# Later scatters and sums, an expert matrix in seven pieces, one gather moved up

## Chip, core and metric

One core of one Trainium2 chip runs the whole program in one launch. The metric is the device time of the run in microseconds (us); the median before is 1282.26 us over three runs (1281.8 to 1287.79).

## What is computed

Three layers in a row, on 4608 tokens of width 512. The gate weights are scaled so that the routing decides clearly.

```python
# 1. attention inside chunks of 64 positions, 8 heads of 64, softmax, no mask
scores = scale * q_c @ k_c.T;  x = softmax(scores) @ v_c         # -> x: 4608 x 512
# 2. dense layer
h = np.maximum(x @ w_in, 0.0);  x = h * h @ w_out                # 512 -> 2048 -> 512
# 3. one of 8 experts for each token
logits = x @ w_gate + modality_bias[modality_id]
e_idx = np.argmax(logits, axis=1);  gate_w = softmax(logits)[e_idx]
for e in range(8):
    mask = e_idx == e
    h = np.maximum(x[mask] @ w1[e], 0.0)                         # 512 -> 1024
    out[mask] = gate_w[mask, None] * (h @ w2[e])                 # 1024 -> 512
```

## The kernel before

**Numbers.** Every fp32 value of a matmul is split into a high and a low fp16 part, and a product is three fp16 matmuls: high by high, high by low, low by high. ScalarE writes the high part, and VectorE or GpSimd the low part as a difference. Most 2 x 2 blocked products go in seven block products instead of eight, so sums and differences of blocks are formed first.

**Stages.** The 4608 tokens are 36 tiles of 128. Nine groups (`supers`) of four tiles go through the dense layer: a first matmul (`mm1` for the first three groups, `prod` for the six others, L620), squares (`square`, whose low part is GpSimd's at L662), and a second matmul in four quarters for each tile (`mm2`, L809), which reads the squares in `bigs[2]` and the weights `w_out` in `bigs[1]`. Attention of the coming tiles runs beside it. Then 25 to 32 pairs, each of 256 tokens of one expert, run through `pair_mm1` (L1189) and `pair_mm2` (L1257). Pair 0's first matmul (`first1`) is slipped between the quarters of the last two tiles.

**Routing.** Behind each tile's last quarter a chain of calls has planned offsets: `x2_evac`; `x2_tr` (a DMA transpose at L829 and a store to DRAM, both on SyncE's queue); `route_a` (a small matmul `lp`, L837, on the transposed tile, then the expert of each token); `route_b` (places within the expert); `route_c`, which computes the gate weight on VectorE and ends with an indirect DMA (L879) on GpSimd's queue that scatters token number and weight into the DRAM table `meta`. Behind tile 31 (`SEEN - 1`), `map_a1`, `meta_gather` and `map_a2` make the index lists of the first four pairs from the tiles seen so far; behind tile 35, `map_b1` to `map_b3` make those of the rest.

**Expert weights.** The two most used experts' matrices are made ready during the dense layer: 16 blocks, each with four quarters loaded into `raw`, seven splits (`part_split`, in the order of `ORDER`), four sums or differences of quarters on GpSimd (`part_sum`, L310) that overwrite a quarter already split, and fourteen stores into the DRAM table `wsp`. `part_plan` writes the list `order_` with times; the splits are 3.43 planned us apart ((742.1 - 96 - 262)/112). The items are emitted strictly in the order of the list, each when it is due and the engines' planned backlog is low; the sum that reads a quarter's last value is followed by the split of the result.

**Hand-over.** After the last quarter of tile 35 the first expert's second matrix (x = 1, 3.67 MB) is loaded from `wsp` into `bigs[1]` by four DMAs that ScalarE issues (`early_w`, L1069): one block, then twice or three times two blocks. Then pair 1's seven first products run (`run1(1, n)`), then pair 0's second matmul, then both kinds alternate, pair 2's first product standing in slot 11. The gather of pair 2 (`x_gather`, L1108, two indirect loads on GpSimd's queue into `bigs[2]`) is emitted at the start of this stage, its two DMA transposes (`x_tr`, L1116, SyncE) in slot 4, its sums (`x_sum0` on VectorE, `x_sum1` on ScalarE and GpSimd) in slots 8 and 10. A slot is one block product, planned at 1.33 us.

**What sets the order.** The program is emitted in one order for all engines by a planner: each step of TensorE advances a planned time T, and before it all events due by T are emitted (`flush`), subject to dependences and to planned backlogs. Each engine then runs its own instructions strictly in that order and waits on semaphores. So where an event is emitted decides what stands behind it in its engine's queue.

Of the kernel before, what the change touches and what calls it, by code (L numbers as in the profile page):

```python
# [12 lines left out]
U32 = mybir.dt.uint32  # L13
AF = mybir.ActivationFunctionType
ALU = mybir.AluOpType
# [7 lines left out]
EARLY = 4  # L23
# [2 lines left out]
FULL = 4  # L26
GSP = 36
WO_O = 4
READY = 2


@with_exitstack
def kernel(
# [18 lines left out]
    NTILE = NT // 128  # L52
# [8 lines left out]
    SEEN = NTILE - 4  # L61
# [16 lines left out]
    meta = dram.tile([MROWS, 2], F32, name="meta")  # L78
    wsp = dram.tile([E, 2, 128, 14336], F16, name="wsp")

    bigs = [big.tile([128, 16384], F16, name=f"big{i}") for i in range(3)]
# [36 lines left out]
    def ts2(out, in0, s1, s2, op0, op1=None, eng=None):  # L118
        if op1 is None:
            (eng or nc.vector).tensor_scalar(out=out, in0=in0, scalar1=s1, scalar2=None, op0=op0)  # L120
        else:
            (eng or nc.vector).tensor_scalar(out=out, in0=in0, scalar1=s1, scalar2=s2, op0=op0, op1=op1)
# [112 lines left out]
    def narrow_hi(which, c):  # L235
        hw = wl[which, c][0]
        if which == 1 and c >= WO_O:
            if "r" not in whp:
# [62 lines left out]
    def part_of(m):  # L301
        return m // (4 * READY), m // 4 % READY, m % 4 * 256

# [9 lines left out]
    SUMS = {0: ((0, 1, 0),), 1: ((1, 2, 1), (2, 2, 0)), 5: ((3, 2, 3),)}  # L313
# [15 lines left out]
    def choose_regs():  # L329
        mp["regs"] = [nc.sync.value_load(first[0:1, k:k + 1], min_val=0, max_val=E - 1) for k in range(READY)]  # L330

# [48 lines left out]
    order_ = []  # L380
# [4 lines left out]
    def part_plan(t0, dt):  # L385
        for m in range(8 * READY):
            t = t0 + 7 * dt * m
            if m == 0:
                order_.extend((t - 8.0 + b, part_load, (m, b)) for b in range(4))
            for n, (k, b) in enumerate(ORDER):  # L390
                at_ = t + n * dt
                order_.append((at_, part_split, (7 * m + n, m, k, b)))
                order_.extend((at_ + 0.3 + 0.1 * x, part_sum, (m, *v, ALU.subtract)) for x, v in enumerate(SUMS.get(n, ())))
                order_.extend((at_ + 0.5 * l + 2.0, part_store, (m, k, l)) for l in range(2))
                nxt = {2: 0, 3: 1, 5: 2, 6: 3}.get(n)
                if nxt is not None and m + 1 < 8 * READY:
                    order_.append((at_ + 3.5, part_load, (m + 1, nxt)))
# [398 lines left out]
    x2 = {}  # L796
# [73 lines left out]
    def route_c(i):  # L870
        a = x2[i]
        di, se = a["di"], a["se"]
        mt = sm_p.tile([128, 2], F32, tag="mt", name="mt")
        nc.gpsimd.tensor_copy(out=mt[:, 0:1], in_=tok[:, i:i + 1])
        ga = sm_p.tile([128, 1], F32, tag="ga", name="ga")
        ts2(ga, se, 1e-9, None, ALU.add)
        nc.vector.reciprocal(out=ga, in_=ga)
        ts2(mt[:, 1:2], ga, a["ui"][:, 0:1], SWG / (SW1 * SW2), ALU.mult, ALU.mult)
        nc.gpsimd.indirect_dma_start(  # L879
            out=meta[:, :], out_offset=bass.IndirectOffsetOnAxis(ap=di[:, 0:1].bitcast(U32), axis=0),  # L880
            in_=mt, in_offset=None,
        )
        x2.pop(i)

    mp = {}
    pair = {}
# [47 lines left out]
    def spread_pairs(ti, fs, base, n):  # L934
        for s in range(n):
            pair[base + s] = [(ti[:, h, s:s + 1], fs[:, h, s:s + 1]) for h in range(2)]
# [79 lines left out]
    def map_a2():  # L1016
        ti, fs = meta_spread(EARLY, "a")
        spread_pairs(ti, fs, 0, EARLY)
        row = const.tile([1, PAIRS], F32, name="row")
        ep = ps_r.tile([128, 512], F32, tag="r", name="epa")  # L1020
        nc.tensor.matmul(ep[0:1, 0:EARLY], lhsT=mp["eha"][:, 0:1], rhs=id_h[:, 0:EARLY], start=True, stop=True)
        nc.vector.tensor_copy(out=row[:, 0:EARLY], in_=ep[0:1, 0:EARLY])
        mp["row"] = row
        mp["rg", 0] = changes(EARLY, "a")
# [42 lines left out]
    def load_part(x, e, k, eng=None, **kw):  # L1067
        a, b = (2048 * n for n in GROUPS[k])
        (eng or nc.sync).dma_start(out=bigs[x][:, a:b], in_=wsp[bass.ds(e, 1), x, :, a:b].rearrange("a p c -> (a p) c"), **kw)  # L1069

    def early_w(x, k):
        assert stored[0] >= 28 * READY * (x + 1), (x, k, stored)
        eng = (nc.sync, nc.scalar)[x]
        if k == 0:
            mp["ew", x] = eng.value_load(mp["rga"][0:1, 0:1], min_val=0, max_val=E - 1)
        load_part(x, mp["ew", x], k, eng)

    def late_w(x, p, n):
        if p >= PAIRS or n not in [b - 1 for _, b in GROUPS] or (x, p, n) in gone:
# [72 lines left out]
    def once(fn, *a):  # L1152
        if a[-1] < PAIRS and (fn, *a) not in gone and a[-1] in pair:
            gone.add((fn, *a))
            fn(*a)
# [152 lines left out]
    def at_time(t, fn, *a):  # L1308
        push(t, [(t, fn, a)], 0)
# [91 lines left out]
    def plan_start():  # L1401
# [53 lines left out]
        for c in range(KF):  # L1455
            op(("old", c), "DMA", 1.35, [("osl", c - 4)], load_w, 1, c)
            op(("ona", c), "ACT", 0.67, [("old", c), ("onb", c - 1), ("nb", KF - 1)] + ([("nr", 3), "nw"] if c >= WO_O else []), narrow_hi, 1, c)
            op(("ond", c), "DVE" if (1, c) in ND_DVE else "ACT", 0.42 if (1, c) in ND_DVE else 0.67, [("old", c)], narrow_lo, 1, c)
# [86 lines left out]
    T = 0.0  # L1545
    span = []
    for su, (b0, nt, sb) in enumerate(supers):
        ta = T
        if su < HALVED:
            for c in range(KF):  # L1550
                steps.append((T, mm1, (su, c)))
                T += STEP
        else:
            for n in range(KF // 4):
                for k in (1, 5, 2, 6, 4, 3, 7):
                    steps.append((T, prod, (su, n, k)))
                    T += STP
        span.append((ta, T))
        TM1 = T
        for t, qq in M2 if su == 0 else [(t, qq) for t in range(nt) for qq in range(4)]:  # L1560
            steps.append((T, mm2, (su, t, qq)))
            T += STEP
            i = b0 + t
            if i >= NTILE - 2 and (i, qq) < (NTILE - 1, 3):
                steps.append((T, first1, (4 * (i - NTILE + 2) + qq,)))
                T += 1.33
            if qq < 3:
                continue
            d = (4.0, 11.0, 16.0, 19.0) if i < NTILE - 1 else (4.0, 8.2, 12.0, 14.0)
            ch = [(T, x2_evac, (i,)), (T + d[0], x2_tr, (i,)), (T + d[1], route_a, (i,)), (T + d[2], route_b, (i,)), (T + d[3], route_c, (i,))]  # L1570
            if i == 3:
                ch += [(T + 22.0, choose, ()), (T + 30.0, choose_regs, ())]
            if i == SEEN - 1:
                ch += [(T + 20.0, map_a1, ()), (T + 23.0, map_a1b, ()), (T + 26.0, meta_gather, (EARLY, "a")), (T + 33.0, meta_turn, (EARLY, "a")), (T + 35.0, map_a2, ())]
                ch += [(T + 37.0 + p, once, (x_gather, p)) for p in range(2)]
                ch += [(T + 44.0 + p, once, (x_tr, p)) for p in range(2)]
                ch += [(T + 49.0 + 8 * p, once, (x_sum, p)) for p in range(2)]
            if i == NTILE - 1:
                ch += [(T + 16.0, map_b1, ()), (T + 18.0, map_b1b, ()), (T + 21.0, map_b2, ()), (T + 22.0, meta_gather, (LATE, "b")), (T + 29.0, meta_turn, (LATE, "b")), (T + 31.0, map_b3, ())]
                ch += [(T + 34.0 + p, once, (x_gather, 4 + p)) for p in range(2)]  # L1580
                ch[1:1] = [(T + 0.1 * k, early_w, (1, k)) for k in range(2, 4)]
                ch[0:0] = [(T, early_w, (1, k)) for k in range(2)]
            at_chain(ch)
        if su == len(supers) - 1:
            at_time(TM1 + 8.0, map_a1c)
            at_time(TM1 + 2.0, rest, "a", [quad(b) for b in range(4)], [slot(n) for n in range(2)])
            for k in range(4):
                at_time(TM1 + 3.0 + 2.65 * k, early_w, 0, k)
            for n in range(7):
                at_time(T - STEP + 1.33 * n, pair_s, 0, n)  # L1590
# [10 lines left out]
    for t, fn, a in plan_start():  # L1601
# [2 lines left out]
    ws = [(87.0 + 9.0 * (3 * q + n), (q, n)) for q in range(4) for n in range(3)] + [(213.0 + 6.0 * q, (q, 3)) for q in range(4)]  # L1604
    at_chain([x for (t, a), (u, b) in zip(ws, [(0.0, None)] + ws[:-1]) for x in ([(u + 4.5, w_split, b)] if b else []) + [(t, w_form, a)]]
             + [(ws[-1][0] + 6.0, w_split, ws[-1][1])])
    for n, (t, _, _) in enumerate(order_):
        at_time(t, part, n)
    with tc.manual_schedule():
# [34 lines left out]
        T = TEND  # L1644
# [43 lines left out]
        slots = []  # L1688
        side = {}

        once(x_gather, 2)
        once(x_gather, 3)
        for k, fn, q in ((4, x_tr, 2), (6, x_tr, 3), (8, x_sum0, 2), (10, x_sum1, 2), (14, x_sum0, 3), (17, x_sum1, 3), (27, x_tr, 4)):
            later(k, fn, q)
        for n in range(7):
            run1(1, n)
# [88 lines left out]
```

## Time and profile before

| | |
|---|---|
| runs | 1287.79, 1282.26, 1281.8 us, median 1282.26 |
| the profiled execution by itself | 1289.27 us, span of the trace 1287.2 us, mean granted TensorE clock 0.972 |
| busy | TensorE 1185.2 us (92%), VectorE 935.0 (73%), ScalarE 707.1 (55%), GpSimd 688.5 (53%) |
| DMA | SyncE's queue q1 117.91 MB, GpSimd's q0 20.54 MB, ScalarE's q10 3.67 MB in 576 packets |

All times in rows are us from the start of the span. PE is TensorE's matmuls, DVE VectorE, ACT ScalarE, POOL GpSimd, SP SyncE; a q behind the name (ACTq, SPq) marks the engine's sequencer issuing a DMA. A helper that records every operation of its kind has one line (L113 all ScalarE activations, L116 most of VectorE's), so tiles tell them apart. In brackets stands how long the engine was idle before an instruction and what ended it. A DMA share over 1 is possible, since packets of several queues overlap.

### The profile page before, as it was taken

The page shows a single profiled execution, that of the slowest core. Times are in us where ns is not written, and L with a number is a line of the kernel's source. Part 1 is how long each engine was busy: PE and PEld are TensorE (multiplying, and loading weights), DVE is VectorE, ACT ScalarE, POOL GpSimd, SP SyncE. Part 2 cuts the span into 40 slices and gives each one's busy share as a digit, 9 for nine tenths or more (in the row PEclk, how much of TensorE's full clock was granted, in tenths as well). Part 3 has the DMA queues.
Part 4 walks back from the last instruction along what each step waited for, and adds up shares of the span by engine and source line. Part 5 has one row for each costly group of instructions (what it writes and reads, how often), then busy time and mean ns, then how long its engine had stood idle before and what let it go on. Part 6 is the DMA issues. An engine that isn't in the chain of part 4 may idle for free. (4 is left out here: it accounts for less than half of the span.)

```text
span 1287.2 us, 33045 instructions
## 1 busy us (share of the span) xinstructions
PE 1185.2 (92%) x12910; PEld 838.3 (65%) x12910; DVE 935.0 (73%) x2031; ACT 707.1 (55%) x1392; POOL 688.5 (53%) x641
## 2 busy tenths in 40 slices
PE   5898999999989989989899899899579999999996
PEld 4443444445754854844764765755569999999995
DVE  6899797775786896885886883943477676766763
ACT  6887673674564664663664562533334555555552
POOL 4488364587573573573483572554145554455451
PEclk9899999999999999999999999999889999999999
DMA  9454523315325437436336423253925435843332
GB/s 375 151 167 129 119 50 96 63 41 124 80 71 128 114 80 156 114 99 147 95 83 162 89 67 93 64 166 74 168 41 117 91 77 163 232 92 75 85 92 58
DMA packets 188775, 144.45 MB, mean 112 GB/s; under 512 B 126586, under 2 KB 163486, under 8 KB 187058
## 3 DMA queue, kind: packets, MB, share of 16 engines
q1 hardware_dynamic: 180386, 117.91, 38.3%
q0 software_dynamic: 7632, 20.54, 5.7%
q10 hardware_dynamic: 576, 3.67, 1.1%
q8 instruction: 103, 1.69, 0.6%
q14 instruction: 78, 0.64, 0.2%
HBM read 204.06 MB, written 34.48 MB: 185 GB/s over the span
## 5 line engine op out<-in xcount | busy, mean ns | idle before, releaser
L809 PEld LDWEIGHTS <-big 128*128 128x128 f16 x1728 | 164.8, 98 | 208.6 <-POOL big L662 15.1
L809 PE MATMUL oo<-big,big 128*128 128x512 f16 x1056 | 237.8, 381 | 3.4 <-POOL big L771 3.4
L1189 PEld LDWEIGHTS <-big 128*128 128x128 f16 x3192 | 192.8, 99 | 22.0 <-issue 17.8
L809 PE MATMUL hh<-big,big 128*128 128x512 f16 x672 | 151.9, 382 | 10.3 <-POOL big L662 10.3
L1189 PE MATMUL hh<-big,big 128*128 128x128 f16 x2040 | 129.2, 220 | 9.7 <-DMA big<-big 9.7
L620 PEld LDWEIGHTS <-big 128*128 128x128 f16 x1152 | 113.5, 100 | 29.9 <-issue 14.1
L791 PE MATMUL hh<-xtall,big 128*128 128x512 f16 x576 | 129.7, 383 | 0.2 <-ACT r L113 0.2
L791 PEld LDWEIGHTS <-big 128*128 128x128 f16 x576 | 55.3, 98 | 64.6 <-issue 2.7
L116 DVE SCALAR_TENSOR_TENSOR stage<-raw,stage 128x256 f16<-128x256 f32 x112 | 76.7, 689 | 20.3 <-ACT stage L113 14.5
L310 POOL TENSOR_TENSOR raw<-raw 128x256 f32<-128x256 f32 x64 | 53.5, 836 | 67.4 <-DVE stage L116 47.6
L1257 PEld LDWEIGHTS <-xtall 128*128 128x128 f16 x840 | 80.4, 99 | 12.1 <-issue 3.1
L488 POOL TENSOR_TENSOR ee<-ee,rc 128x512 f32<-128x512 f32 x36 | 40.2, 1117 | 84.2 <-DVE rc L486 58.2
L1283 POOL DMA_INDIRECT out_dram<-raw,tib x30 | 35.2, 1172 | 92.3 <-DVE raw L116 73.2
L879 POOL DMA_INDIRECT meta<-mt,di x36 | 37.6, 1046 | 85.4 <-issue 27.2
L771 POOL TENSOR_TENSOR big<-sn,big 128x512 f16<-128x512 f32 x48 | 59.0, 1233 | 35.9 <-DVE sn L116 15.7
L1257 PE MATMUL oo<-big,xtall 128*128 128x256 f16 x600 | 75.4, 277 | 2.7 <-DVE raw L116 2.7
L662 POOL TENSOR_TENSOR big<-r,big 128x512 f16<-128x512 f32 x48 | 65.3, 1375 | 17.5 <-ACT big L113 9.7
L1150 POOL TENSOR_TENSOR big<-big 128x512 f16<-128x512 f32 x34 | 39.5, 1181 | 60.8 <-ACT big L113 60.7
L116 DVE SCALAR_TENSOR_TENSOR qkt<-qk,qkt 128x1024 f16<-128x1024 f32 x32 | 51.5, 1608 | 21.7 <-ACT qkt L113 21.2
L113 ACT ACTIVATE big<-hh 128x512 f32<-128x512 f32 x62 | 36.8, 594 | 53.7 <-PE hh L1189 46.3
L662 POOL TENSOR_TENSOR big<-sn,big 128x512 f16<-128x512 f32 x48 | 60.0, 1265 | 11.5 <-ACT big L113 10.1
L113 ACT ACTIVATE stage<-raw 128x256 f16<-128x256 f32 x112 | 45.4, 409 | 35.7 <-DMA wsp<-stage 18.5
(384 smaller groups left out, 2705.9 us busy)
## 6 DMA issues: line engine op xcount, KB each, us to landing
big<-wsp SPq DMA_DIRECT2D x111, 1024.0 KB
big<-wsp SPq DMA_DIRECT2D x37, 512.0 KB
qk<-in_qk_dram SPq DMA_DIRECT2D x34, 512.0 KB
wsp<-stage SPq DMA_DIRECT2D x224, 64.0 KB
x2d<-xs SPq DMA_DIRECT2D x36, 256.0 KB
vv<-in_v_dram SPq DMA_DIRECT2D x34, 256.0 KB
big<-in_w_in_dram SPq DMA_DIRECT2D x16, 512.0 KB
raw<-in_w_out_dram SPq DMA_DIRECT2D x16, 512.0 KB
```

Source lines behind the costliest of these rows:

```text
L113: nc.scalar.activation(out=out, in_=in_, func=func, **kw)
L116: nc.vector.scalar_tensor_tensor(out=out, in0=in0, scalar=s, in1=in1, op0=op0, op1=op1, **kw)
L310: nc.gpsimd.tensor_tensor(out=quad(out_), in0=quad(in0), in1=quad(in1), op=op)
L488: eng.tensor_tensor(out=ee, in0=ee, in1=rc.unsqueeze(2).to_broadcast([128, H, 64]), op=ALU.mult)
L620: nc.tensor.matmul(ps[:, f * 256:f * 256 + 256], lhsT=block(k, la, kk, 2 * n + f), rhs=xa(lb, kk), start=k in (1, 5, 2, 4) and f + m + kk ...
L662: nc.gpsimd.tensor_tensor(out=lo, in0=c, in1=hi, op=ALU.subtract)
L771: nc.gpsimd.tensor_tensor(out=lo, in0=q32.rearrange("p (f n) -> p f n", f=nf), in1=hi, op=ALU.subtract)
L791: nc.tensor.matmul(hp[:, q_ * n:(q_ + 1) * n], lhsT=wi[:, la, kk, f * 128:f * 128 + 128], rhs=x[:, lb, kk, :], start=i == 0, stop=i == 3 * ...
L809: nc.tensor.matmul(ps, lhsT=g[:, la, f, c:c + 128], rhs=wo[:, lb, f, :], start=f == 0 and n == 0, stop=f == KF - 1 and n == 2)
L1150: eng.tensor_tensor(out=sl[:, 2 * h:2 * h + 2], in0=s[h], in1=sh[:, 2 * h:2 * h + 2], op=ALU.subtract)
L1189: nc.tensor.matmul(ps[:, f * 128:f * 128 + 128], lhsT=WB[0][:, n, la, kk, f * 128:f * 128 + 128], rhs=xa(lb, kk), start=first and f + m + ...
L1257: nc.tensor.matmul(ps, lhsT=hb[:, la, f * 128:f * 128 + 128], rhs=WB[1][:, n, lb, f, :], start=first and f + m == 0, stop=True, skip_group ...
```

## The change

- `part_sum` is planned 2.2 us (a second one 3.3) behind its split instead of 0.3 (0.4), and the list `order_` is sorted by time.
- The scatter leaves `route_c` and becomes `route_d`, an event of its own: 6 planned us behind `route_c` for most tiles, 2 for tile 34, 0.2 for tile 31, 0.5 for tile 35.
- The second expert matrix is loaded in seven DMAs of one block each, in the order 0, 4, 1, 5, 2, 6, 3: two behind each of the first three quarters of tile 35 (`EW` = 0.8 planned us later) and one behind the last. Blocks 0 and 4 lie on the parts of `w_out` that the first quarter reads last, and so on.
- Pair 2's gather is emitted 0.5 and its transposes 6.5 planned us behind the first quarter of tile 35.
- `map_a2` goes 2 us later, and its second half, the rows that tell when an expert changes, becomes `map_a2b`, 10 us behind it; the gathers of pairs 0 and 1 go 1.5 us later.

```diff
+EW = 0.8
-                order_.extend((at_ + 0.3 + 0.1 * x, part_sum, (m, *v, ALU.subtract)) for x, v in enumerate(SUMS.get(n, ())))
+                order_.extend((at_ + 2.2 + 1.1 * x, part_sum, (m, *v, ALU.subtract)) for x, v in enumerate(SUMS.get(n, ())))
...
+    def route_d(i):
+        a = x2.pop(i)
         nc.gpsimd.indirect_dma_start(
-            out=meta[:, :], out_offset=bass.IndirectOffsetOnAxis(ap=di[:, 0:1].bitcast(U32), axis=0),
-            in_=mt, in_offset=None,
+            out=meta[:, :], out_offset=bass.IndirectOffsetOnAxis(ap=a["di"][:, 0:1].bitcast(U32), axis=0),
+            in_=a["mt"], in_offset=None,
         )
-        x2.pop(i)
...
         spread_pairs(ti, fs, 0, EARLY)
+
+    def map_a2b():
         row = const.tile([1, PAIRS], F32, name="row")
...
-        load_part(x, mp["ew", x], k, eng)
+        if x == 0:
+            load_part(x, mp["ew", x], k, eng)
+            return
+        a, e = (0, 4, 1, 5, 2, 6, 3)[k] * 2048, mp["ew", x]
+        eng.dma_start(out=bigs[x][:, a:a + 2048], in_=wsp[bass.ds(e, 1), x, :, a:a + 2048].rearrange("a p c -> (a p) c"))
...
+            if i == NTILE - 1 and qq < 3:
+                for k in range(2):
+                    at_time(T + EW + 0.1 * k, early_w, 1, 2 * qq + k)
+                if qq == 0:
+                    at_time(T + 0.5, once, x_gather, 2)
+                    at_time(T + 6.5, once, x_tr, 2)
             if qq < 3:
                 continue
-            d = (4.0, 11.0, 16.0, 19.0) if i < NTILE - 1 else (4.0, 8.2, 12.0, 14.0)
+            d = (4.0, 11.0, 16.0, 19.0, 25.0) if i < NTILE - 2 and i != SEEN - 1 else (4.0, 11.0, 16.0, 19.0, 21.0) if i < NTILE - 1 and i != SEEN - 1 else (4.0, 11.0, 16.0, 19.0, 19.2) if i < NTILE - 1 else (4.0, 8.2, 12.0, 14.0, 14.5)
...
-                ch[1:1] = [(T + 0.1 * k, early_w, (1, k)) for k in range(2, 4)]
-                ch[0:0] = [(T, early_w, (1, k)) for k in range(2)]
+                ch[1:1] = [(T + 0.1, early_w, (1, 6))]
...
+    order_.sort(key=lambda e: e[0])
...
-        once(x_gather, 2)
         once(x_gather, 3)
-        for k, fn, q in ((4, x_tr, 2), (6, x_tr, 3), (8, x_sum0, 2), (10, x_sum1, 2), (14, x_sum0, 3), (17, x_sum1, 3), (27, x_tr, 4)):
+        for k, fn, q in ((6, x_tr, 3), (8, x_sum0, 2), (10, x_sum1, 2), (14, x_sum0, 3), (17, x_sum1, 3), (27, x_tr, 4)):
```

## Rows read from the trace of the kernel before

**Rows 1.** Busy time by stretches: start:end, length, engines, PEclk, DMA share, GB/s.

```profile
880.00:892.00 12.00, 12.00 (x120) 7.75 (x119) 4.92 (x19) 3.33 (x9) 1.24 (x2) 1.00 0.01 2
892.00:896.00 4.00, 4.00 (x38) 2.58 (x37) 1.62 (x9) 1.45 (x4) 0.82 (x1) 1.00 0.52 131
902.00:912.00 10.00, 5.59 (x100) 5.47 (x99) 6.14 (x18) 3.06 (x7) 1.39 (x1) 0.94 0.90 305
912.00:917.00 5.00, 5.00 (x48) 5.00 (x48) 3.12 (x7) 3.91 (x9) 1.88 (x3) 0.50 1.49 185
917.00:934.00 17.00, 7.32 (x85) 6.60 (x83) 3.10 (x11) 2.94 (x7) 1.94 (x2) 0.80 1.16 74
980.00:1250.00 270.00, 270.00 (x3671) 256.15 (x3669) 192.82 (x335) 151.15 (x281) 138.82 (x119) 1.00 0.47 114
```

**Rows 2.** Timeline of PE, 880 to 950: start, us, line, operation [idle before].

```profile
887.36 2.75 PE L809 MATMUL oo<-big,big 128*128 128x512 f16 x12
...
899.20 0.35 PE L837 MATMUL lp<-wgs,x2t 128*128 128x16 f16 x8
...
904.72 1.50 PE L1189 MATMUL s_all<-qkt,big 128*128 128x128 f16 x24
...
911.97 0.37 PE L1189 MATMUL hh<-vv,big 128*128 128x128 f16 x2 [4.41 <-ACT big L113]
...
918.85 0.17 PE L837 MATMUL lp<-wgs,x2t 128*128 128x16 f16 x1
...
934.06 2.72 PE L1189 MATMUL hh<-big,big 128*128 128x128 f16 x24 [9.74 <-DMA big<-big]
...
948.68 0.18 PE L1058 MATMUL ep<-id_h,ehb 128*1 128x21 f16 x1 [3.27 <-DVE rj L116]
```

**Rows 3.** Timeline of ACT, 904 to 912.

```profile
904.66 0.34 ACTq L1069 DMA_DIRECT2D big<-wsp  x1
...
910.93 0.34 ACTq L1069 DMA_DIRECT2D big<-wsp  x1
911.32 0.60 ACT L113 ACTIVATE big<-hh 128x512 f32<-128x512 f32 x1 [5.11 <-DMA big<-wsp]
```

**Rows 4.** Timeline of POOL, 895 to 897.

```profile
895.18 1.00 POOL L879 DMA_INDIRECT meta<-mt,di  x1 [12.20 <-DVE mt L122]
...
896.48 0.99 POOL L1108 DMA_INDIRECT big<-x2d,tia  x1 [0.30 <-issue]
```

**Rows 5.** Timeline of SP, 891 to 924.

```profile
891.20 1.23 SPq L829 DMA_TRANSPOSE x2t<-xs  x1
...
906.44 1.37 SPq L829 DMA_TRANSPOSE x2t<-xs  x1
...
908.54 15.80 SPq L1116 DMA_TRANSPOSE big<-big  x2
```

**Rows 6.** DMA issues, whole span: count, median us from issue to landing.

```profile
big<-x2d,tia POOLq DMA_INDIRECT x4, 4.7
```

**Rows 7.** Timeline of DVE at 934.

```profile
934.04 0.69 DVE L1135 TENSOR_TENSOR big<-big 128x512 f32<-128x512 f16 x1 [11.83 <-DMA big<-big]
```

**Rows 8.** Timelines of POOL, ACT and PE around 457 and 560 to 574.

```profile
455.25 1.02 POOL L879 DMA_INDIRECT meta<-mt,di  x1 [3.67 <-issue]
...
457.08 0.42 ACT L113 ACTIVATE stage<-raw 128x256 f16<-128x256 f32 x1 [3.27 <-POOL raw L310]
...
459.96 2.48 PE L620 MATMUL oo<-xtall,pt 128*128 128x256 f16 x12 [2.94 <-ACT r L113]
...
557.99 0.99 POOL L879 DMA_INDIRECT meta<-mt,di  x1 [3.73 <-issue]
...
573.54 10.15 PE L809 MATMUL hh<-big,big 128*128 128x512 f16 x40 [2.97 <-POOL big L662]
```

**Rows 9.** Waits, summed over the span: us in total, times, longest.

```profile
POOL raw L310 <- DVE stage L116: 47.6, 20, 9.6
...
ACT stage L113 <- POOL raw L310: 16.1, 7, 5.1
```

More of the change, by code (lines that the diff above doesn't have):

```diff
@@ L878, in route_c @@
         ts2(mt[:, 1:2], ga, a["ui"][:, 0:1], SWG / (SW1 * SW2), ALU.mult, ALU.mult)
+        a["mt"] = mt
+    def route_d(i):
+        a = x2.pop(i)
         nc.gpsimd.indirect_dma_start(
-            out=meta[:, :], out_offset=bass.IndirectOffsetOnAxis(ap=di[:, 0:1].bitcast(U32), axis=0),
-            in_=mt, in_offset=None,
+            out=meta[:, :], out_offset=bass.IndirectOffsetOnAxis(ap=a["di"][:, 0:1].bitcast(U32), axis=0),
+            in_=a["mt"], in_offset=None,
         )
-        x2.pop(i)
     mp = {}
@@ L1566 @@
                 T += 1.33
+            if i == NTILE - 1 and qq < 3:
[4 more added lines that the diff above has]
+                    at_time(T + 6.5, once, x_tr, 2)
             if qq < 3:
                 continue
-            d = (4.0, 11.0, 16.0, 19.0) if i < NTILE - 1 else (4.0, 8.2, 12.0, 14.0)
-            ch = [(T, x2_evac, (i,)), (T + d[0], x2_tr, (i,)), (T + d[1], route_a, (i,)), (T + d[2], route_b, (i,)), (T + d[3], route_c, (i,))]
+            d = (4.0, 11.0, 16.0, 19.0, 25.0) if i < NTILE - 2 and i != SEEN - 1 else (4.0, 11.0, 16.0, 19.0, 21.0) if i < NTILE - 1 and i != SEEN - 1 else (4.0, 11.0, 16.0, 19.0, 19.2) if i < NTILE - 1 else (4.0, 8.2, 12.0, 14.0, 14.5)
+            ch = [(T, x2_evac, (i,)), (T + d[0], x2_tr, (i,)), (T + d[1], route_a, (i,)), (T + d[2], route_b, (i,)), (T + d[3], route_c, (i,)), (T + d[4], route_d, (i,))]
             if i == 3:
@@ L1573 @@
             if i == SEEN - 1:
-                ch += [(T + 20.0, map_a1, ()), (T + 23.0, map_a1b, ()), (T + 26.0, meta_gather, (EARLY, "a")), (T + 33.0, meta_turn, (EARLY, "a")), (T + 35.0, map_a2, ())]
-                ch += [(T + 37.0 + p, once, (x_gather, p)) for p in range(2)]
+                ch += [(T + 20.0, map_a1, ()), (T + 23.0, map_a1b, ()), (T + 26.0, meta_gather, (EARLY, "a")), (T + 33.0, meta_turn, (EARLY, "a")), (T + 37.0, map_a2, ())]
+                ch += [(T + 38.5 + p, once, (x_gather, p)) for p in range(2)]
                 ch += [(T + 44.0 + p, once, (x_tr, p)) for p in range(2)]
-                ch += [(T + 49.0 + 8 * p, once, (x_sum, p)) for p in range(2)]
+                ch += [(T + 47.0, map_a2b, ())] + [(T + 49.0 + 8 * p, once, (x_sum, p)) for p in range(2)]
             if i == NTILE - 1:
```

## The prediction

> **What bounds the kernel now.** I read the busy time by stretches first, then TensorE's idle gaps in order of time, then what ended each gap, engine by engine. From 980 to 1250 us TensorE is busy for 270.00 of 270 us at full clock [rows 1]: the pair loop can give nothing, whatever is done to the other engines. So the change is worth what it does to the gaps before it. The densest ones lie between 902 and 950 us, where the last dense tile hands over to the expert pairs. There TensorE stops twice for long: 4.41 us until 911.97 for a PSUM bank that ScalarE had not copied, and 9.74 us until 934.06 for a transpose of the third pair [rows 2]. Behind each stop it runs at the lower of its two clock levels: granted 0.50 (1.2 GHz) over 912 to 917 [rows 1], and the 24 matmuls at 934.06 took 2.72 us where 24 of the same shape took 1.50 at 904.72 [rows 2].
>
> Both stops come from transfers. ScalarE issues the second expert matrix (3.67 MB in four pieces) only after the last dense tile; the fourth piece is held until 910.93, and the copy behind it starts at 911.32 after 5.11 us of idleness [rows 3]. The transfers run at 305 GB/s over 902 to 912, and the transposes behind them still fill 917 to 934, though only 74 GB/s move [rows 1]. The DMA engines had been empty before: share 0.01 from 880 to 892. The third pair's gather waited on GpSimd behind the scatter of tile 33, which sat 12.20 us until VectorE had its values; it left at 896.48 [rows 4], and its first transpose at 908.54, behind that of the last tile [rows 5].
>
> **The change part by part.**
>
> *Third pair's gather and transposes.* The gather now stands on GpSimd's queue behind the first quarter of the last tile's second matmul, which ends at 887.36 + 2.75 = 890.1 [rows 2], and ahead of tile 33's scatter, whose emission goes to 6 planned us later. It leaves 6.4 us earlier. Its second half follows 1.3 us later, as 896.48 followed 895.18 [rows 4], and lands in 4.7 [rows 6], so the transposes can be issued at about 897 instead of 908.54. On SyncE they now pass the last tile's transpose (906.44 [rows 5]). TensorE wants them at 924.3, less the 4.41 and 2.24 us that go in the next two steps: at 917.7. From 897 to there are 20 us; the same pair of transposes took 25.5 now (908.54 to 934.06), mostly behind other transfers. I take the whole stop as gone: **+9.74** (bounds: 25.5 us again would land it at 922.5 and leave 4.8, so +4.9 to +9.74).
>
> *Second expert matrix in seven pieces.* Pieces 0 and 4 can go once the first quarter is done (890.1), two more after each further quarter, the last at 902. Three instructions more on ScalarE at 0.34 each [rows 3] make 1.0 us beside its idle time there; I count nothing. At 305 GB/s 3.67 MB need 12 us, and from 890 to 902 there are 12, so at 902 little is outstanding where 3.67 MB were. The hold on ScalarE goes: **+4.41** (bounds -8.8, three holds for one, to +4.41; the row nearest is the third issue at 904.66, which passed with 1.5 MB outstanding, as much as the new order ever has if it drains at that rate).
>
> *Clock.* Without the two stops the clock should stay up: 5.00 busy us of 912 to 917 would be 5.00 x 1.50/2.72 = 2.76, so 2.24 back, and 1.22 at 934.06: **+3.46** (bounds 0 to 3.46).
>
> *VectorE's backlog.* It stood 11.83 us before the third pair's sums [rows 7] with the routing of the last tile and the pair map queued behind; TensorE then waited 3.27 us for the map at 948.68 [rows 2]. The map's chain of small instructions stays, the backlog doesn't: **+1.5** (0 to 3.27).
>
> *What the earlier transfers hit.* The routing matmuls stand in TensorE's queue and want the transposes of tiles 34 and 35. Tile 34's was issued at 891.20 [rows 5] on empty DMA engines, whose traffic was a share of 0.52 over 892 to 896 [rows 1], and nothing waited at 899.20 [rows 2]. Tile 35's, among the matrix's pieces, took from 906.44 until at most 918.85, 12.4 us. Now tile 34's is the one among pieces: with 12.4 us it lands at 903.6, and TensorE waits 4.4. Tile 35's matmul moves to 918.85 - 4.41 - 2.24 = 912.2; if it still takes 12.4 us, 6.6 are lost. Between 0 and -11.0 I take **-2.5**: pieces of half the size, in pairs with room between, but a third pair's transposes in front.
>
> By the Trainium skill, "DMA: Bandwidth & Descriptors", section "Queues, rings and completion order", each DMA engine takes turns between the queues that have work, a packet at a time. Tile 35's 12.4 us beside ScalarE's queue agree with that; the slow transposes of 917 to 934, with little else moving, are not explained by it. Taken strictly it speaks against the change: it is the first rival's mechanism.
>
> *Scatters later* (36 of them, mostly 6 planned us). A scatter that waits on GpSimd holds all behind it. Two cases [rows 8]: at 455.25 one had waited 3.67 us, the sum of expert weights behind it ran late, ScalarE's split of that quarter began at 457.08 after 3.27 us, and TensorE stood 2.94 us at 459.96. At 557.99 one had waited 3.73 us, GpSimd then ran without a pause, and TensorE stood 2.97 us at 573.54 for a square. Together 5.91; other scatters I bound by as much again, so 0 to +11.8. As the work behind may not be ready earlier either, I take **+4**.
>
> *Sums later.* Emitted with the store of the split, not with the split itself, a sum no longer makes GpSimd wait for VectorE (47.6 us over 20 waits [rows 9]). But the last sum of each block was planned 3.13 us ahead of the split that reads it and is now 1.23 ahead (2.2 after one split, at a step of 3.43). ScalarE already waits for sums 16.1 us over 7 times [rows 9]. If that doubles and half of the new waits reach TensorE, 7 to 8 us go; if GpSimd's freed time reaches it, 3 come. I take **-1**. The sort of the list puts a load behind the next split instead of before it, the same instructions on the same queue: nothing. The map's rows for the weight switch (one tiny matmul and five small VectorE instructions) move 10 planned us; a like matmul waited 3.27 [rows 2], so at most that either way, taken as nothing, since the other engines' work around it stays.
>
> **Sum.** 9.74 + 4.41 + 3.46 + 1.5 - 2.5 + 4 - 1 = 19.6 us. The profiled execution took 1289.27 us by itself, 7.0 over the median of 1282.26; it would become 1269.7. If the 7.0 lie elsewhere, the median becomes 1262.7; if they lie in the stops removed, 1269.7. I put a third of them there: **1265 us**. Its own range is 1253 to 1273.
>
> **Rivals.**
>
> *1. The wait moves to the routing matmuls.* The transposes of tiles 34 and 35 lose turns to the pieces and to the third pair's transposes, 11.0 us instead of 2.5. For it: the 12.4 us of tile 35, and the slow transposes after 917. Against: DMA engines empty until 892, and the pieces halved. Gain 11.1, less the third of the offset (2.3): 1273.5.
>
> *2. ScalarE is held three times instead of once.* Each pair of pieces finds the queue full and holds the copies behind it for 4.41 us of TensorE. For it: the hold at 910.93. Against: the third issue passed. 13.2 us off the sum leave 6.4, less 2.3: 1278.
>
> *3. Slower: the late sum stalls ScalarE in every block.* Place: the last split of each of the 16 blocks, which reads the quarter just summed, with 1.23 planned us between; a GpSimd busy with squares runs the sum too late, ScalarE stands before the split, and the copies of PSUM behind it hold TensorE, 2.94 us each as at 459.96. For it: the chain of the first case [rows 8] is exactly this. Against: only 7 waits now, and most of them cost TensorE nothing. The other terms give 20.6, so it is slower by over 0.5% from the tenth block on ((20.6 + 6.4)/2.94 = 9.2). At 12 blocks it costs 35.3: 1297 us.
>
> **How the numbers follow.** Forecast 0.68, rivals 0.13, 0.10 and 0.09. 0.5%, which is about what a measurement of this kernel tells from no change, is 6.4 us: faster means below 1275.8. The forecast is faster, the first rival for 0.10 of its 0.13, the second is no change: 0.78, 0.13 and 0.09. The range runs from 1252 (scatters at 11.8 and the map at 3.27) to 1280 (the second rival in); above it lies the third rival, so about 2 in 10 with the ends of the others.
>
> **What would show it.** Right: the third pair's gather just after the last tile's first quarter, its transposes landed before TensorE's first matmul on them, no ScalarE gap behind a weight issue, full clock from 905 to the end of the map, GpSimd's idle time before scatters far under what it is. Wrong in the single step: a TensorE gap ahead of a routing matmul (first rival); ScalarE gaps between 890 and 902 (second); more and longer waits of ScalarE's splits for the sums, with gaps in the products before 840 (third). The forecast falls if the stretch from 880 to 980 gets less than 10 us shorter.

## The result and the profile after

The changed kernel takes 1269.3 us (1266.4 to 1271.93), the kernel before 1282.03 in the same comparison: a ratio of 0.9895, 95% interval [0.9852, 0.9938]. That is 12.7 us faster and 4 us over the forecast, inside its range. The profiled executions stand 22.9 us apart (1266.40 and 1289.27), since that of after was the fastest of its four and that of before was slower than any of the four runs of this comparison. So what a part is worth is taken below from medians, and the traces say only where the time went.

The pair loop is as before: 270.00 busy us of 270. The hand-over isn't as forecast. The same matmul of tile 32's routing, before and after:

```profile
879.25 0.17 PE L857 MATMUL rp<-run,ones_h 128*128 128x8 f16 x1
```

```profile
860.89 0.17 PE L858 MATMUL rp<-run,ones_h 128*128 128x8 f16 x1
```

From there to the end of the span (1287.2 and 1264.7 us) only 4.1 us are saved; 18.4 of the 22.5 between the two traces lie ahead of it. By the prediction's own sign (less than 10 us from 880 to 980) its forecast falls, though its time held.

Windows of after, with the columns of [rows 1]:

```profile
874.00:889.00 15.00, 15.00 (x187) 11.28 (x185) 8.18 (x29) 5.12 (x11) 3.40 (x3) 1.00 1.10 181
889.00:901.00 12.00, 0.20 (x4) 0.08 (x2) 1.78 (x7) 0.27 (x1) 0.00 (x0) 0.66 1.18 222
901.00:906.00 5.00, 4.62 (x44) 4.62 (x44) 2.83 (x7) 4.24 (x10) 1.28 (x2) 0.50 0.53 141
...
960.00:1230.00 270.00, 270.00 (x3670) 256.15 (x3669) 192.81 (x335) 147.42 (x277) 138.53 (x119) 1.00 0.46 114
```

TensorE stands from 889 to 901, and then runs at 0.50 (1.2 GHz), as it did behind the old stops. Its timeline (answers to [rows 2]) names ScalarE:

```profile
901.38 0.37 PE L1199 MATMUL hh<-vv,big 128*128 128x128 f16 x2 [12.18 <-ACT big L114]
...
903.89 2.73 PE L1199 MATMUL s_all<-qkt,big 128*128 128x128 f16 x24
...
925.61 0.17 PE L1064 MATMUL ep<-id_h,ehb 128*1 128x21 f16 x1 [3.27 <-DVE rj L117]
```

The stop of 9.74 us for pair 2's transposes is gone. The stop of 4.41 behind ScalarE has become one of 12.18, and the map still makes TensorE wait 3.27. ScalarE's timeline (answers to [rows 3]):

```profile
875.45 0.91 ACTq L1086 DMA_DIRECT2D big<-wsp  x2
...
877.26 1.01 ACTq L1086 DMA_DIRECT2D big<-wsp  x2
...
882.67 0.86 ACTq L1086 DMA_DIRECT2D big<-wsp  x2
...
900.35 0.34 ACTq L1086 DMA_DIRECT2D big<-wsp  x1
900.73 0.60 ACT L114 ACTIVATE big<-hh 128x512 f32<-128x512 f32 x1 [12.88 <-DMA big<-big]
```

Six pieces left without a hold; the seventh stood until 900.35, and the copy that TensorE wanted stood behind it. Read the bracket: before, such a copy waited for `big<-wsp`, a piece of the matrix; now for `big<-big`. Those are pair 2's transposes, which SyncE had issued at 874.88, just ahead of the pieces. GpSimd's gather for them and SyncE's issues (answers to [rows 4, 5]):

```profile
870.52 0.97 POOL L1118 DMA_INDIRECT big<-x2d,tia  x1 [3.10 <-PE oo L810]
```

```profile
874.88 7.50 SPq L1126 DMA_TRANSPOSE big<-big  x2
...
888.10 8.69 SPq L830 DMA_TRANSPOSE x2t<-xs  x1
```

So they took 25.5 us from issue to the release (874.88 to 900.35), the bad end that the prediction had given them.

Ahead of the hand-over, GpSimd's wait for the splits fell as forecast and ScalarE's for the sums grew; neither was priced right (answers to [rows 9]):

```profile
POOL raw L311 <- DVE stage L117: 23.8, 17, 4.1
...
ACT stage L114 <- POOL raw L311: 26.5, 12, 5.1
```

### The profile page after: what moved, and what is told of

Same layout as the page of the kernel before. It is cut to its first block, busy times and chain, and to the rows that moved or that the text cites. A ratio compares the mean times of both kernels' runs of the same rounds, so it can differ in the third digit from the quotient of the medians.

```text
span 1264.7 us, 33052 instructions
## 1 busy us (share of the span) xinstructions
PE 1173.8 (93%) x12910; PEld 833.9 (66%) x12910; DVE 917.6 (73%) x2031; ACT 706.6 (56%) x1392; POOL 690.6 (55%) x641
## 5 line engine op out<-in xcount | busy, mean ns | idle before, releaser
L117 DVE SCALAR_TENSOR_TENSOR stage<-raw,stage 128x256 f16<-128x256 f32 x112 | 73.6, 660 | 41.9 <-ACT stage L114 36.7
L772 POOL TENSOR_TENSOR big<-sn,big 128x512 f16<-128x512 f32 x48 | 59.4, 1242 | 32.4 <-DVE sn L117 16.1
L663 POOL TENSOR_TENSOR big<-r,big 128x512 f16<-128x512 f32 x48 | 61.6, 1295 | 26.1 <-ACT big L114 24.1
L117 DVE SCALAR_TENSOR_TENSOR qkt<-qk,qkt 128x1024 f16<-128x1024 f32 x32 | 47.2, 1475 | 17.3 <-ACT qkt L114 16.8
L884 POOL DMA_INDIRECT meta<-mt,di x36 | 42.2, 1172 | 22.5 <-issue 10.2
```

Source lines behind the costliest of these rows:

```text
L117: nc.vector.scalar_tensor_tensor(out=out, in0=in0, scalar=s, in1=in1, op0=op0, op1=op1, **kw)
L663: nc.gpsimd.tensor_tensor(out=lo, in0=c, in1=hi, op=ALU.subtract)
L772: nc.gpsimd.tensor_tensor(out=lo, in0=q32.rearrange("p (f n) -> p f n", f=nf), in1=hi, op=ALU.subtract)
L884: nc.gpsimd.indirect_dma_start(out=meta[:, :], out_offset=bass.IndirectOffsetOnAxis(ap=a["di"][:, 0:1].bitcast(U32), axis=0), in_=a["mt"], ...
```

## The experiments

**Theory.** One part of the change is harmful: pair 2's transposes among the pieces are slow there, and by a shared completion semaphore they hold an instruction that has nothing to do with them. (A completion semaphore is the counter that a DMA raises when its bytes have landed.) **Rival.** ScalarE is held by too many bytes outstanding, so that pieces beside the dense layer's last quarters cost it whatever stands with them. Beside this: which parts bring the time.

The program as built gives the DMAs of SyncE and ScalarE eight completion semaphores, and a DMA that gets one in use waits until that one's earlier DMA has landed. The order and number of DMAs ahead decide who shares with whom. In the built program of after, the second piece waits for semaphore 6, last raised by the store of tile 32, and the last piece for semaphore 5, which pair 2's second transpose raises. In that of before, the fourth piece waits for the second.

By the Trainium skill, "DMA: Bandwidth & Descriptors", section "Why a DMA increments its semaphore by 16 and not by 1", two DMAs in flight on one semaphore can pass a wait before the first has landed, which is a reason for such waits. No run here shows that, since each waits.

| kernel | median us | ratio to before, 95% | TensorE idle, 870 to 960 |
|---|---|---|---|
| before (range over all comparisons 1275 to 1289) | 1283.6 to 1284.1 | | 23.2 |
| e1 scatters alone | 1289.93 | 1.0042 [1.0016, 1.0068] | 15.7 |
| e2 sums and sort alone | 1268.02 | 0.9882 [0.9843, 0.9922] | 16.5 |
| e3 map alone | 1280.29 | 0.9979 [0.9958, 1.0] | 17.3 |
| e4 seven pieces alone | 1268.56 | 0.9888 [0.9859, 0.9917] | 8.8 |
| e5 gather and transposes alone | 1272.43 | 0.9911 [0.9882, 0.9941] | 9.1 |
| e6 after, last piece later | 1261.96 | 0.9845 [0.9802, 0.9888] | 15.6 |
| e7 sort alone | 1274.62 | 0.994 [0.9914, 0.9967] | 14.6 |
| e8 sums, sort, map, pieces | 1255.58 | 0.9799 [0.9764, 0.9835] | 8.4 |
| f1 after, transposes put back | 1258.1 | 0.9788 [0.9761, 0.9816] | 12.2 |
| f2 e8 and scatters | 1258.28 | 0.9798 [0.9771, 0.9824] | 8.3 |
| f3 e8 and gather moved up | 1255.84 | 0.9773 [0.9746, 0.98] | 8.3 |
| f4 late sums, not sorted | 1303.09 | 1.0147 [1.0119, 1.0176] | 28.0 |

The last column is 90 us less TensorE's busy time from 870 to 960 in the one profiled execution (after: 19.8). After was timed in an earlier comparison (0.9895, 1269.3); beside these ratios its difference to a kernel can come out 1 to 3 us other than from the medians.

**e4, the pieces alone.** The whole edit of `early_w` (seven DMAs, two behind each of tile 35's first three quarters, one behind the last), on the kernel before.

> The kernel before with the second expert matrix in seven pieces alone; the third pair's gather and transposes stay where they were. In the build each DMA shares its completion semaphore with an earlier one and waits for that one; here the last piece shares with the first piece, which has long landed. Theory C (ScalarE's hold is that wait): no hold of ScalarE behind the last piece, TensorE's 4.41 us stop gone, the stop for the third pair's transposes 3 to 9 us: 6 to 12 us faster, about 1273. Theory D (the issuing queue is full, whoever landed): ScalarE held for 4 us or more at the last piece, TensorE's stops together 12 us or more: within 3 us of before.

It brings 15 us, more than the 6 to 12 of theory C, whose mechanism it shows. The last piece shares its semaphore with the first, long landed, and leaves with nothing idle behind it:

```profile
901.21 0.34 ACTq L1081 DMA_DIRECT2D big<-wsp  x1
901.65 0.59 ACT L114 ACTIVATE big<-hh 128x512 f32<-128x512 f32 x1
```

Pair 2's transposes, issued 905.06, now come behind the pieces, and TensorE's wait for them is gone too. So the pieces take away both stops of [rows 2], and the gather need not move.

**e5, the gather and transposes alone.**

```diff
+            if i == NTILE - 1 and qq == 0:
+                at_time(T + 0.5, once, x_gather, 2)
+                at_time(T + 6.5, once, x_tr, 2)
...
-        once(x_gather, 2)
```

> The kernel before with one part: pair 2's gather and transposes moved up, the matrix still in four pieces. In this program the fourth piece has the same completion semaphore as the second of pair 2's transposes, so it can't be issued until that has landed; before, it waited for the second piece. Theory A (the hold is that shared semaphore): the transposes leave about 10 us earlier, before any piece, but in the changed kernel such a pair needed 25 us beside pieces; if it needs that here, ScalarE is held until about 913 (5 us, as before) and only the stop of 9.74 us goes: 1272 us. If it lands before 903, no hold is left either and 1268 us follow. Theory B (the hold is the bytes outstanding on ScalarE's queue): the gather changes nothing there, the hold stays at 4.4 us, and the fourth piece leaves when the second has landed: 1273 us. The trace tells them apart by what lands just before the fourth piece leaves.

It brings 11.7 us (1272.43), which by itself fits both theories; the trace decides. Timelines of ScalarE, SyncE and TensorE, then the windows behind the transposes' issue:

```profile
902.26 0.34 ACTq L1069 DMA_DIRECT2D big<-wsp  x1
902.69 0.59 ACT L113 ACTIVATE big<-hh 128x512 f32<-128x512 f32 x1
902.77 0.67 ACTq L1069 DMA_DIRECT2D big<-wsp  x1
```

```profile
890.89 3.13 SPq L1116 DMA_TRANSPOSE big<-big  x2
```

```profile
914.33 0.38 PE L837 MATMUL lp<-wgs,x2t 128*128 128x16 f16 x8 [4.32 <-DMA x2t<-xs]
```

```profile
894.00:896.00 2.00, 2.00 (x18) 1.17 (x17) 0.00 (x0) 0.00 (x0) 0.07 (x1) 1.00 0.72 131
896.00:898.00 2.00, 2.00 (x31) 1.48 (x28) 0.91 (x2) 0.19 (x1) 0.00 (x0) 1.00 0.06 8
```

Two readings. The fourth piece leaves 0.51 us behind the third, and ScalarE's queue had moved only 1.42 MB by 905 of the 2.6 in the three pieces ahead of it: that rules out bytes outstanding as the cause of the hold. And the DMA engines are nearly idle from 896 (0.06) and idle from 898, so the same transposes that took 25.5 us among pieces take at most 7.1 without. No hold is left, yet the 1268 us of that case don't come: in place of the hold TensorE waits for tile 35's transpose, which now stands among four pieces: the first rival's mechanism, at 4.32 us.

**e6, after with the last piece later.**

```diff
-                ch[1:1] = [(T + 0.1, early_w, (1, 6))]
             at_chain(ch)
+            if i == NTILE - 1:
+                at_time(T + 6.0, early_w, 1, 6)
```

> The changed kernel with one step moved: the seventh piece is emitted 6 planned us behind the last quarter of tile 35 instead of 0.1, after tile 35's own transpose; nothing else. By that it shares its completion semaphore with a weight load that landed long before, not with the second of pair 2's transposes. Theory A (shared semaphore): ScalarE's idle time of 12.88 us and TensorE's of 12.18 at 889 to 901 go; the time falls from 1269.4 to about 1257 us (1254 to 1262). Theory B (too many bytes outstanding): the piece is held as long, or holds later copies for as long, and the time stays at 1267 to 1270.

The hold goes as the theory says: the piece leaves at 896.80, and ScalarE works on. But only 7.3 of the 12 us come (medians), so the time stands at the slow end of theory A. SyncE, and what TensorE waits for:

```profile
888.19 2.46 SPq L1075 DMA_DIRECT2D big<-wsp  x2
903.79 1.25 SPq L830 DMA_TRANSPOSE x2t<-xs  x1
```

```profile
906.91 0.38 PE L838 MATMUL lp<-wgs,x2t 128*128 128x16 f16 x8 [10.17 <-DMA x2t<-xs]
```

With one DMA fewer ahead, tile 35's transpose is the one that gets semaphore 5, and SyncE holds it until pair 2's transposes have landed. The slow transposes hold whoever shares with them.

**f1, after with pair 2's transposes in slot 4 again.**

```diff
-                    at_time(T + 6.5, once, x_tr, 2)
...
-        for k, fn, q in ((6, x_tr, 3), (8, x_sum0, 2),
+        for k, fn, q in ((4, x_tr, 2), (6, x_tr, 3), (8, x_sum0, 2),
```

> The changed kernel with one step put back: pair 2's two transposes stand in slot 4 again, behind all seven pieces, while its gather stays moved up, and the scatters stay late. The seventh piece then has the same semaphore as the first. Theory A (the transposes among the pieces are what costs: they take 25 us there, and the seventh piece waits for them): no hold of ScalarE behind the seventh piece, the transposes issued at about 890 land in under 10 us, no stop of TensorE for them, and about 12 us less than the changed kernel: 1257 us (1254 to 1261). Theory B (pieces beside the dense layer's last copies hold ScalarE whatever stands beside them): the hold of 12 us stays, 1267 to 1270.

1258.1 against 1269.3: one call moved back is worth 11 us (13.7 by the ratios to before). The hold is gone, and of waits for a transpose 0.2 us are left. Moving the transposes was the harmful part.

**f3, the same without the late scatters; e8, also without the gather moved up; f2, e8 with the scatters.**

> The kernel before with three parts (later sums with sort, the split of the map, the matrix in seven pieces), without the later scatters and without the gather moved up. Theory A (scatters cost 5 us, and the gather moved up only brings the hold of 12 us): the parts add but for the hand-over they share. With the sums alone TensorE's gaps from 880 to 960 were 16.5 us, with the pieces alone 8.8, so 7.7 us and some 2 of clock come on top of 1268.0, and about 3 of the map: 1256 us (1252 to 1261), and no hold of ScalarE at the pieces, since the seventh waits only for the first. Theory B (the parts give the same gain in different ways): 1266 us or more, like each of them alone.

> The changed kernel without the late scatters and with pair 2's transposes in slot 4; its gather stays moved up. Against the kernel without the gather moved up (1255.6) only the gather's place differs. Theory A (TensorE no longer waits for pair 2 at all once the pieces are out of the way, so an earlier gather gives nothing): 1254 to 1257 us. Theory B (an earlier gather is worth something by itself, as the squares of VectorE behind pair 2's sums begin earlier): 1252 us or less. Theory C (the gather ahead of tile 33's scatter holds GpSimd): 1259 or more.

> The changed kernel without the gather and transposes moved up, so with the late scatters, the late sums, the split map and the pieces. Against the kernel without both (1255.6) only the scatters differ. Theory A (scatters cost in company what they cost alone, 5 us, by later squares on GpSimd): 1259 to 1262 us, with more waiting of TensorE for the squares' low part between tiles 8 and 28 than the 3.6 us it has without. Theory B (with the sums out of the way the scatters have nothing to hold up, so neither place costs): 1254 to 1257.

e8 came out as added up beforehand, 1255.6. f3 is the same: an earlier gather by itself gives nothing. f2's median lies between its two theories, and its ratio is e8's, so over the whole span the scatters cost nothing that can be told apart. They do act, though. Windows from tile 8's routing matmul to tile 28's and from there to tile 32's, of e8 and of f2, which differ in the scatters alone:

```profile
317.32:775.39 458.07, 428.98 (x4640) 287.53 (x4639) 362.22 (x838) 267.32 (x563) 270.25 (x253) 0.99 0.46 110
775.39:863.54 88.15, 80.71 (x612) 54.14 (x611) 56.71 (x173) 36.48 (x72) 47.78 (x50) 1.00 0.44 113
```

```profile
317.23:781.02 463.79, 431.57 (x4639) 289.22 (x4638) 361.96 (x838) 266.86 (x563) 266.68 (x253) 0.98 0.47 109
781.02:863.35 82.33, 80.43 (x612) 54.25 (x610) 50.12 (x172) 35.17 (x70) 43.41 (x43) 1.00 0.40 115
```

Late scatters cost 5.7 us in the first stretch and give 5.8 back in the second. The other traces with late sums agree: with late scatters 462.3 to 464.3 us and then 82.1 to 83.5 (after, e6, f1), without them 457.8 to 458.1 and then 86.8 to 89.0 (e2, f3). No run moves the scatters of one stretch alone.

e8 and f3 beat both kernels, by 28 us and by 14. A window of f3, where the 80 us of after from 880 have 60.18 busy us at 0.89:

```profile
880.00:960.00 80.00, 71.67 (x929) 64.52 (x928) 60.22 (x157) 37.09 (x73) 34.37 (x31) 0.96 0.47 117
```

**e1, the scatters alone** (the diff's `route_d` and its offsets).

> The kernel before with the later scatters alone (route_d as in the change, nothing else). Theory A (the middle of the span gives a third or more of the gain, because a scatter that waits on GpSimd no longer holds the squares and sums behind it): 3 to 6 us faster, about 1278; GpSimd's idle time ahead of scatters falls from 85.4 us to under 30, and tile 31's routing comes 3 to 6 us earlier. Theory B (the gain is all in the hand-over after the last dense tile; what the two profiled executions differ by before it is variation between executions): within 1.5 us of before.

5 us slower, where 4 us faster had been forecast; neither theory came. GpSimd's idle time ahead of scatters did fall, from 85.4 us to 40.1, but less of it did not make the kernel faster.

**e3, the map alone** (`map_a2b` and the moved calls):

> The kernel before with the map of the first four pairs moved and cut in two alone (map_a2, map_a2b, gathers of pairs 0 and 1). Theory A, as the stretch from tile 31's to tile 32's routing got 10 us shorter: 5 to 9 us faster, about 1275, with the TensorE waits of 4.11 and 2.35 us in that stretch gone. Theory A': those 10 us come from scatters and sums as well, so less than 2 us here. Theory B: within 1.5 us.

3 us faster (0 to 5), at the edge of what can be told.

**e2, later sums and sort**, and its two halves, **e7** (the sort) and **f4** (the later sums):

```diff
-  (at_ + 0.3 + 0.1 * x, part_sum, ...)
+  (at_ + 2.2 + 1.1 * x, part_sum, ...)
...
+    order_.sort(key=lambda e: e[0])
```

> The kernel before with the later sums and the sorted list alone. Theory A: 0 to 4 us faster, GpSimd's wait for VectorE ahead of sums falls from 47.6 us to about half. Theory B: within 1.5 us. Third rival of the prediction (the late sum stalls ScalarE): ScalarE's wait for sums rises over 30 us and the kernel is slower by 5 us or more.

> The kernel before with the list of loads, splits, sums and stores sorted by planned time, but the sums planned as before (0.3 and 0.1, not 2.2 and 1.1). Against the kernel with later sums and sort, SyncE's order is the same, TensorE's nearly (21 lines), and GpSimd's differs. Theory A (the sort makes the gain of that kernel, since it changes the order of loads, stores and TensorE's work): 1268 us (1263 to 1273). Theory B (the sums make it, since GpSimd no longer waits 47.6 us for VectorE's splits): 1281 us or more, and GpSimd's wait for VectorE at the sums stays near 47.

> The kernel before with later sums (2.2 and 1.1 planned us), but the list left as it was, not sorted. Sorting alone gave 9.5 us, both together 15.5. Theory A (the sums are worth the other 6 us by themselves, through GpSimd's waits for the splits, 47.6 us before): 1278 us (1275 to 1281). Theory B (the late sum needs the sort, since in the unsorted list a sum that is due late keeps all splits behind it from being emitted): 1282 us or more.

The sort alone brings 9.5 us (7.7 by the ratio), between its two theories; both together bring 15.5, which none of e2's theories had; and the later sums without the sort cost 19, by theory B. Windows from tile 8's routing matmul to tile 28's, the same work in each, of before, e1, e7 and e2:

```profile
317.06:787.04 469.98, 435.01 (x4640) 289.82 (x4639) 365.79 (x835) 265.70 (x560) 266.50 (x251) 0.97 0.46 107
```

```profile
316.01:789.50 473.49, 436.81 (x4640) 289.00 (x4639) 369.88 (x835) 265.57 (x560) 263.00 (x251) 0.97 0.45 106
```

```profile
316.69:781.86 465.17, 432.36 (x4640) 288.01 (x4638) 358.44 (x838) 267.11 (x563) 270.15 (x253) 0.98 0.46 108
```

```profile
317.57:775.41 457.84, 428.73 (x4640) 287.36 (x4639) 362.26 (x838) 267.15 (x563) 269.59 (x253) 0.99 0.45 110
```

From before to e2 the stretch is 12.1 us shorter. Half of it is waiting (469.98 - 435.01 = 35.0 against 29.1), the other half the same 4640 matmul rows in 6.3 us less, since behind fewer stops the clock is granted higher (0.97 to 0.99). Of the 5.9 us less of waiting, 5.4 are waits for GpSimd's low part of the squares. In e1 that wait is 4.7 us longer than before, but all waits together only 1.7 (36.7 against 35.0). Before, e1 and e2:

```profile
PE hh L809 <- POOL big L662: 10.1, 8, 3.0
```

```profile
PE hh L809 <- POOL big L662: 14.8, 5, 4.0
```

```profile
PE hh L809 <- POOL big L662: 4.7, 6, 2.3
```

And how far the preparation of the expert weights reaches, by its last split on ScalarE, in before, e7, e2 and f4:

```profile
828.19 0.42 ACT L113 ACTIVATE stage<-raw 128x256 f16<-128x256 f32 x1 [1.12 <-POOL raw L310]
```

```profile
811.95 0.42 ACT L113 ACTIVATE stage<-raw 128x256 f16<-128x256 f32 x1 [1.09 <-POOL raw L310]
```

```profile
807.10 0.42 ACT L113 ACTIVATE stage<-raw 128x256 f16<-128x256 f32 x1 [2.69 <-POOL raw L310]
```

```profile
879.65 0.42 ACT L113 ACTIVATE stage<-raw 128x256 f16<-128x256 f32 x1 [6.58 <-DMA wsp<-stage]
```

The list is emitted strictly in its order. Unsorted, an item with a late time keeps earlier ones behind it; sorted, the whole stream ends 16 us sooner in the traces. With the sums made later and no sort it gets worse: the splits run 51 us longer, up to the hand-over, and TensorE stands 16.77 us for tile 32's transpose. That the order of the list is the reason is read from the code and these ends; no run changed it in another way.

## Why the prediction was right or wrong

The time was right by luck: two large errors cancelled, and the place of the gain was wrong.

- **ScalarE's hold, +4.41:** wrong. It became 12.18, so this term was -7.8. The step that failed is "The hold on ScalarE goes", which priced bytes outstanding (1.5 MB, the third issue); e5 shows that bytes did not hold it. The hold of before was the fourth piece waiting for the second by a shared semaphore.
- **Third pair's transposes, +9.74:** the stop is gone, as said, and the 25.5 us that stood as a bound came true. The reading that little else moved beside the slow transposes of before was wrong: from 917 to 934 ScalarE's queue, with the fourth piece, moved 0.84 of the 1.26 MB (last section). What failed is "leave 4.8" beside it: it charged slow transposes to the TensorE matmul that reads them, not to an unrelated piece of ScalarE. And e4 has the same gain without the move; the part by itself costs 11 us in the changed kernel (f1).
- **Sums, -1, and the sort, "nothing":** wrong. They bring 15.5 alone, the sort by itself 9.5. No run takes them out of the changed kernel; in e8 and f3 the stretch from tile 8 to 28 is as short as in e2, in after 4.5 us longer, with the late scatters. The prediction looked at what each instruction waits for; it counted the sort as "the same instructions on the same queue" and did not ask when the planner may emit them.
- **Scatters, +4:** wrong sign alone (+5.4 us of time, e1), and in company a loss and a gain that cancel (f2 against e8). The bounds of 0 to 11.8 left out a loss with no reason for it. Why the first stretch gets longer stays open.
- **Clock, +3.46, and VectorE's backlog, +1.5:** not had in the hand-over of after (0.50 over 901 to 906; 3.27 at 925.61). Between tiles 8 and 28 the same matmuls do take less, 430.15 us in after against 435.01 (428.73 in e2), in a stretch that the prediction had not priced.
- **Routing matmuls, -2.5:** no such wait shows in after, where the hold covers it; 4.32 us in e5, none in e8. The mechanism was right in e5, where tile 35's transpose stands among four pieces. The 10.17 us in e6 are another one's, the shared semaphore.
- **Map, nothing:** 0 to 5 us (e3).
- **Rivals:** the second named the right place, with one long hold in place of three short ones and another cause. The third is not seen in after: ScalarE does wait longer for sums (26.5 us against 16.1), but TensorE's waits between tiles 8 and 28 fell (32.1 us against 35.0). A loss of its size came only in f4, and not by its mechanism: there ScalarE waits 11.5 us for the sums, less than before.

## What to carry to other kernels

Before moving a DMA, list what each DMA waits for. Where a program deals a few completion semaphores to many DMAs, the semaphore's earlier user is among it: a slow transfer holds whichever engine's next DMA gets the same one, and that engine's work with it. Keep DMA transposes out of a stretch in which bulk copies run; here that was worth 11 us. And where one list is emitted in order, its sorting is a change of its own, to be priced and measured apart from the edit that made it necessary.

## What was not expected of the hardware

- The same two transposes (each 128 x 1024 in fp16) took at most 7.1 us on empty DMA engines (e5) and 25.5 us among pieces (after). The pieces suffer too. DMA queues of before, ScalarE's (q10) over 902 to 912, then SyncE's (q1, with the transposes) and ScalarE's over 917 to 934 (packets, MB, share of the 16 engines' time):

```profile
q10 hardware_dynamic: 408, 2.47, 68.0%
```

```profile
q1 hardware_dynamic: 1578, 0.40, 83.7%
q10 hardware_dynamic: 117, 0.84, 30.8%
```

ScalarE's queue falls from 247 to 49 GB/s beside the transposes. Why both are so slow together stays open.
- One VectorE instruction on 128 x 8 int32 took 4.04 us before and 0.17 after. Timelines of VectorE before, GpSimd before, VectorE after:

```profile
827.47 4.04 DVE L120 TENSOR_SCALAR ci<-ci 128x8 int32<-128x8 int32 x1
```

```profile
827.42 0.73 POOL L310 TENSOR_TENSOR raw<-raw 128x256 f32<-128x256 f32 x1
828.11 2.27 POOL L662 TENSOR_TENSOR big<-r,big 128x512 f16<-128x512 f32 x2
830.34 1.15 POOL L662 TENSOR_TENSOR big<-sn,big 128x512 f16<-128x512 f32 x1
```

```profile
817.92 0.17 DVE L121 TENSOR_SCALAR ci<-ci 128x8 int32<-128x8 int32 x1
```

It ends at 831.51, when GpSimd's unbroken run ends (831.49). By the Trainium skill, "Trainium Architecture — The Big Picture", section "What this means for kernel authors", VectorE and GpSimd share a port pair that one of them holds at a time; these rows agree, though other VectorE instructions run beside GpSimd unhindered, and no run was made to test it.
